# A fused attention and feed-forward kernel whose whole hand-recorded order, engine choice and buffer table are replaced by another

## The chip, the cores and the metric

The kernel runs on one core of one Trainium2 chip. The metric is the device time of one execution in microseconds (us); the profile's span runs from the first to the last instruction of the program. Five engines work side by side, each in its own order: PE (TensorE, matmuls), DVE (VectorE), ACT (ScalarE), POOL (GpSimd) and SP (SyncE, which here only issues DMAs). An engine never overtakes in its own queue: an instruction that waits holds up everything behind it on that engine.

## What is computed

Four batches with four heads of 1088 tokens (head size 32) go through an attention whose feature map is a product of two 8-row sketches, without softmax; the result, 4352 tokens of 128 values, goes through a two-layer network with a PReLU of 2048 channels.

```python
def phi(x):
    a = np.einsum('rd,bhsd->bhsr', S1, x)
    b = np.einsum('rd,bhsd->bhsr', S2, x)
    return np.einsum('bhsi,bhsj->bhsij', a, b).reshape(*x.shape[:-1], r * r)
q_p, k_p = (phi(q), phi(k))
kv = np.einsum('bhsf,bhsd->bhfd', k_p, v)
z = np.sum(k_p, axis=2)
num = np.einsum('bhsf,bhfd->bhsd', q_p, kv)
den = np.einsum('bhsf,bhf->bhs', q_p, z)[..., None] + 1e-06
x = (num / den)                      # 4352 tokens x 128
h = x @ w_in
g = np.maximum(h, 0.0) + alpha * np.minimum(h, 0.0)
out = g @ w_out
```

## The kernel before

The class `Graph` (line 43) makes a list of named steps; each has the engines on which it may run, the steps that it needs and its buffers. Nothing is scheduled when the kernel runs: the string `ORDER` (line 664) lists every step as `name@engine` (p PE, d DVE, a ACT, g POOL, s SP) and the loop at the end emits them in that order, so that each engine gets its own steps in the order of the string. `SLOTS` (line 655) says which of its class's buffers (PSUM banks among them) each logical buffer uses. Waits follow from the data and from buffers that are used again.

```python
    for word in ORDER.split():
        name, _, e = word.partition("@")
        if name in ("fill", "bit"):
            G.dummy(int(e), 512 if name == "fill" else 128)
            continue
        G.names[name].emit(E[e])
```

The names that the text uses, with b the batch (0 to 3):

- Loads on SP: `ld.kb.x`, `ld.qb.x`, `ld.vb.0` to `ld.vb.3` (keys, queries, values), `ld.w_in0` to `3` and `ld.w_out0` to `3` (weights, 256 KB each). A load into a padded or reused tile waits for a small memset first: `vpadb` (line 154) ahead of all loads of vb, `kpadb` (line 156) ahead of one load of kb, `hold.*` (line 159).
- Keys, `keys` (line 315 on): `kbT` transposes them (DVE, line 323), `kbf` is the sketch matmul, `kbab` transposes its result into the tile kab (DVE, line 333), `kbp..` are the key products, four for a batch (one a head, 576 wide; for batch 0 eight, of 320 or 256) on POOL or DVE into the tiles kp (line 134), `kbv` multiplies them with the values (PE), and `kbvc`, `kbvT`, `kbW` lead to the table kvW. `kbzm`, `kbcw`, `kbcc` make the denominator's weights fW.
- Queries: the first 512 tokens of batch 0 take a short way (`f0`, `f1`, line 397 on; tiles aq, dt, rr; `f0.x` writes the first activations xT). The others go `qbT`, `qbf` (PE), `qbg` (DVE, tile gt), `qbcb`, `qbs`, `qbe`, `qbrc`, `qbbd` (the denominator, tile dn), the four query products `qbp00` to `qbp11` (512 wide, POOL or DVE, tiles pr), two transposes `qbt0`, `qbt1` (DVE, line 480, tile pt), the numerators' matmul `qbn` (PE, tiles pt and kvW) and `qbx0`, `qbx2` (to xT).
- Weights, `weights` (line 268): `w_in_bf` casts; `w_a`, `w_b`, `w_hi`, `w_lo` (tiles wb, w_hl) make the PReLU's scaled copies of w_out; `winT`, `winTc`, `Wmm`, `W` make the product of both layers that carries alpha.
- The network, `mlp` (line 532): token blocks 0a, 0b (256 tokens), 1 to 6 (512) and 7 to 9 (256). For each of 16 channel chunks c: `hB.c` (PE, first layer into one PSUM bank), `rB.c` (relu to bf16 into one of ten rh tiles, ACT line 550 or DVE line 552), `oB.c` (PE, second layer); `WB` adds the alpha product, `tB` takes the result out, `sB` stores it. Blocks 7 to 9 are taken out by plain copies into the tiles oL, E and kvF.
- `warm`, `fill` and `bit` are matmuls on constants whose result nobody reads.

Blocks 0a, 0b and 1 hold batch 0; blocks 2 and 3 come out of q1 (batch 1), 4 and 5 out of q2, 6, 8 and 9 out of q3 and 7 out of the tokens left over in all batches.

Of the kernel before, what the change touches and what calls it, by code (L numbers as in the profile page):

```python
# [663 lines left out]
ORDER = """  # L664
ld.k0.0@s ld.rows1@s kpad0@g vpad2@g ld.k0.1@s ident@g mask4@d amkp@d par2@d q32@d hold.q2@g ld.w_in1@s k0T0@d zero@d ld.rows0@a warm@p ld.q0.0@s
amkq@d ld.w_in0@s identb@g M8T@g fill@2 bit@2 rowsT@p kW@d ld.alpha@a k0T1@d hold.k1@d hold.q1@d fill@5 bit@1 k0f@p am@g table@a aT@p fW@d Sab1@a
w_in_bf1@a M8@d E8@g ld.w_out0@s Sab0@d Mz@d alphaT@a hold.k2@d vpad1@g ld.w_out1@s k0ab@d k0z@p vpad0@g kpad2@g q0T0@d bit@3 f0.a@p ld.v0.0@s f0.b@p
k0zm@d omaT@d k0p02@g ld.v0.1@s w_in_bf0@a f0.ac@a k0p00@d k0p03@d k0p10@d fill@1 bit@1 winT0@p ld.v0.2@s ld.v0.3@s ld.w_in3@s k0p12@d k0fz@p S1x@p
hold.qr@d f0.m@d k0p01@g w_b1@d k0zz@d w_a0@a k0p11@g S1rep@d k0p13@g f1.a@p winTc0@a k0zc@d f1.b@p w_hi1@a bit@3 f0.den@p f1.ac@d ld.q0.1@s
ld.w_in2@s f0.dT@d w_in_bf3@a ld.k1.0@s ld.w_out3@s w_b0@g k0v0@p k0cw@p f1.m@d q0T1@d k0v1@p k0Vc@d kpad1@g f0.e@a w_hi0@a f0.rc@d w_lo1@g f1.den@p  # L670
k0vc@a w_a1@g ld.k1.1@s k0VT@p ld.w_out2@s w_in_bf2@a k0vT@p f1.dT@d k0V@d w_lo0@g f0.num@p k0cc@d ld.v2.0@s f0.rr@d f0.x@d q0f@p h0a.6@p q0g@d
ld.k2.0@s ld.k3.0@s q0cb@g ld.v3.1@s winT1@p ld.q1.0@s h0a.4@p ld.v1.1@s w_b3@g h0a.12@p k1T0@d ld.k2.1@s ld.v2.2@s f1.e@a w_a3@a r0a.6@a ld.k3.1@s
ld.v3.2@s k0W@a ld.v1.3@s ld.q2.0@s ld.v1.0@s h0a.14@p r0a.4@a f1.rc@d r0a.12@a winTc1@a w_hi3@a f1.rr@d o0a.6@p f1.num@p q0s@d f1.x@d w_b2@g k1f@p
o0a.12@p h0a.10@p k1ab@d o0a.4@p h0b.8@p h0a.8@p k1z@p w_hi2@a h0b.2@p h0b.12@p q0e@g q0rc@d w_a2@g r0a.14@d r0a.8@a o0a.14@p h0a.2@p k1zm@d w_lo2@d
r0b.8@a q0bd@d w_lo3@d h0b.6@p q0p01@d h0b.14@p o0a.8@p r0a.2@a h0a.0@p o0a.2@p r0a.10@a q0p00@g r0a.0@a r0b.12@a Wmm@p r0b.2@a r0b.6@a o0a.0@p
o0a.10@p h0b.0@p q1T@d h0b.10@p q0t0@d ld.v1.2@s ld.v2.1@s W_lo@a r0b.14@a k1cw@p W@d k2T0@d r0b.0@a r0b.10@a q0n@p W0a@p q0x0@a k2f@p k1cc@d t0a@d
k2ab@d q1f@p q1g@d o0b.14@p k1p00@g k1p01@g k1p03@g k1p02@g h1.0@p o0b.0@p k2p03@d o0b.6@p q1cb@d h0b.4@p h1.11@p W0b@p o0b.10@p h1.12@p r0b.4@a
r1.0@a h1.2@p h1.10@p h1.7@p r1.7@a h1.4@p ld.v2.3@s ld.q3.0@s k2p02@g k2p01@g o0b.8@p q1s@d o0b.4@p r1.4@d q1e@a r1.12@a h1.5@p q1rc@d h1.8@p
o0b.12@p o0b.2@p q3T@d r1.5@a q1bd@g r1.8@a q1p01@g t0b@d k2z@p k1v0@p h1.3@p h1.6@p q2T@d q1p11@d q1p00@d q1p10@d r1.11@a o1.11@p h1.14@p k2zm@d
# [90 lines left out]
```

## Time and profile before

| | us |
|---|---|
| median of 3 runs | 110.03 (109.38 to 110.6) |
| the profiled execution | 110.21 |
| its span | 108.3 |
| PE busy | 97.3 (90%) |
| DVE busy | 84.1 (78%) |
| ACT busy | 69.8 (64%) |
| POOL busy | 43.0 (40%) |

Instructions, their durations and what ended a wait are read from the timeline; a row `x2` merges neighbours. Matmuls overlap (each is shown with its time through the array), so PE's progress is read from the starts of two neighbours. The view by stages gives each engine's busy time between two moments. The last part of the chain of waits names only PE for most of the span, from 44.69 us to 103.91 us.

### The profile page before, as it was taken

How to read it: one execution, taken by the hardware profiler on the slowest of the kernel's cores; microseconds unless marked ns; L12 is line 12 of the kernel's file. 1: busy time of each engine (PE TensorE's matmuls, PEld its weight loads, DVE VectorE, ACT ScalarE, POOL GpSimd, SP SyncE). 2: the span in 40 equal slices, each digit the busy share in tenths (PEclk: the TensorE clock that was granted, in tenths of full speed). 3: DMA queues.
4: the chain of work that ended last, by engine and by line, in shares of the span. 5: the costliest groups of instructions: out<-in, count | busy, mean ns of one | idle time of the engine just before them, and what ended most of it. 6: DMA issues, size and time to landing. Idle time of an engine off the chain costs nothing.

```text
span 108.3 us, 3658 instructions
## 1 busy us (share of the span) xinstructions
PE 97.3 (90%) x1522; PEld 57.3 (53%) x1533; DVE 84.1 (78%) x151; ACT 69.8 (64%) x139; POOL 43.0 (40%) x58
## 2 busy tenths in 40 slices
PE   7998487899799899799999999999999999999950
PEld 2456254458646654544444444444644446699940
DVE  2499978879989999989978893779794594894810
ACT  3159666999924799338696448762994695658520
POOL 5449692856978380002960940026800230000000
PEclk9999999999999999999999999999999999999997
DMA  2897679997950000000510523250111000027333
GB/s 81 244 334 196 190 255 376 402 328 210 319 197 3 0 9 0 6 0 6 97 24 4 108 45 91 48 97 0 29 28 29 0 0 6 0 49 121 72 62 99
DMA packets 21730, 11.28 MB, mean 104 GB/s; under 512 B 16192, under 2 KB 19024, under 8 KB 21712
## 3 DMA queue, kind: packets, MB, share of 16 engines
q1 hardware_dynamic: 20808, 10.82, 35.7%
q10 hardware_dynamic: 904, 0.21, 0.8%
q8 instruction: 12, 0.20, 0.8%
q14 instruction: 6, 0.05, 0.1%
HBM read 8.80 MB, written 2.23 MB: 102 GB/s over the span
## 4 chain that ended last, share of the span: by engine, by line
PE 57%; DVE 21%; DMA 9%; issue 4%; POOL 3%; ACT 2%; SPq 1%; ACTq 1%; DVEq 0%
PE ps L137 56%; DMA w_out_f<-in_moe_w_out_dram 5%; DMA k<-in_k_dram 3%; DVE pt__78 L480 2%; DVE kp__70 L134 2%; DVE kT__64 L323 2%; DVE pr__76 L134 2%; POOL kp__69 L134 1%; POOL pr__75 L134 1%; DVE kp__69 L134 1%; DVE dn__80 L134 1%; DVE gt__73 L451 1%; DVE qT__72 L509 1%; DVE qT__71 L509 1%; ACT w_a L278 1%
## 5 line engine op out<-in xcount | busy, mean ns | idle before, releaser
L137 PEld LDWEIGHTS <-w_in_bf 128*128 128x128 bf16 x176 | 16.7, 98 | 13.0 <-issue 2.1
L137 PE MATMUL ps<-xT__103,w_in_bf 128*128 128x256 bf16 (+1 forms) x94 | 22.2, 325 | 0.4 <-issue 0.2
L137 PEld LDWEIGHTS <-w_a 128*128 128x128 bf16 x128 | 12.2, 98 | 12.4 <-issue 2.6
L137 PE MATMUL ps<-xT__104,w_in_bf 128*128 128x256 bf16 (+1 forms) x63 | 15.5, 325 | 0.2 <-issue 0.2
L550 ACT ACTIVATE rh__89<-ps 128x512 bf16<-128x512 f32 x16 | 9.6, 602 | 7.2 <-PE ps L137 7.0
L134 POOL TENSOR_TENSOR kp__69<-kab__66 128x576 f32<-128x576 f32 (+1 forms) x9 | 10.8, 1222 | 4.2 <-DVE kab__66 L333 4.2
L550 ACT ACTIVATE rh__88<-ps 128x512 bf16<-128x512 f32 x15 | 9.1, 605 | 3.5 <-PE ps L137 3.4
L550 ACT ACTIVATE rh__92<-ps 128x512 bf16<-128x512 f32 x13 | 7.9, 610 | 1.6 <-PE ps L137 1.4
L134 POOL TENSOR_TENSOR pr__75<-gt__73 128x512 f32<-128x512 f32 x7 | 7.8, 1121 | 2.4 <-DVE gt__73 L134 2.0
L134 POOL TENSOR_TENSOR dn__80<-gt__73 128x128 f32<-128x128 f32 (+2 forms) x3 | 1.5, 498 | 18.0 <-DVE gt__73 L451 18.0
L137 PE MATMUL ps<-pt__78,kvW 32*32 32x256 f32 (+2 forms) x320 | 6.9, 332 | 1.2 <-DVE pt__78 L480 0.6
L137 PE MATMUL ps<-const-bfloat16-1.0 128*128 128x512 bf16 (+1 forms) x24 | 6.3, 406 | 0.9 <-PEq L754 0.8
L550 ACT ACTIVATE rh__93<-ps 128x512 bf16<-128x512 f32 x9 | 5.5, 606 | 2.4 <-PE ps L137 2.3
L550 ACT ACTIVATE rh__90<-ps 128x512 bf16<-128x512 f32 x11 | 6.7, 606 | 0.5 <-PE ps L137 0.5
L137 PE MATMUL ps<-rh__88,w_a 128*128 128x512 bf16 (+1 forms) x21 | 6.5, 339 | 0.5 <-ACT rh__88 L550 0.5
L323 DVE STREAM_TRANSPOSE kT__64<-k 128x1152 f32<-128x1152 f32 (+1 forms) x5 | 5.6, 1129 | 1.5 <-DMA k<-in_k_dram 1.4
L137 PE MATMUL ps<-rh__89,w_a 128*128 128x512 bf16 (+1 forms) x21 | 6.1, 328 | 0.3 <-issue 0.2
L451 DVE STREAM_TRANSPOSE gt__73<-ps 128x1024 f32<-128x1024 f32 (+2 forms) x5 | 4.9, 984 | 1.8 <-PE ps L137 1.7
L137 PEld LDWEIGHTS ps<-pt__78,kvW 32*32 32x32 f32 x320 | 4.1, 103 | 3.7 <-DVE pt__78 L480 1.0
L550 ACT ACTIVATE rh__94<-ps 128x512 bf16<-128x512 f32 x9 | 5.6, 623 | 0.4 <-PE ps L137 0.4
L137 PE MATMUL ps<-rh__92,w_a 128*128 128x512 bf16 (+1 forms) x16 | 5.7, 366 | 0.1
L550 ACT ACTIVATE rh__91<-ps 128x512 bf16<-128x512 f32 x9 | 5.5, 609 | 0.3 <-PE ps L137 0.3
(202 smaller groups left out, 231.3 us busy)
## 6 DMA issues: line engine op xcount, KB each, us to landing
v<-in_v_dram SPq DMA_DIRECT2D x12, 144.0 KB, 4.5
q<-in_q_dram SPq DMA_DIRECT2D x3, 512.0 KB, 5.6
k<-in_k_dram SPq DMA_DIRECT2D x4, 288.0 KB, 6.3
k<-in_k_dram SPq DMA_DIRECT2D x4, 256.0 KB, 4.3
w_in_f<-in_moe_w_in_dram SPq DMA_DIRECT2D x4, 256.0 KB, 4.4
w_out_f<-in_moe_w_out_dram SPq DMA_DIRECT2D x4, 256.0 KB, 5.6
out_dram<-oT__100 SPq DMA_DIRECT2D x12, 64.0 KB, 1.9
q<-in_q_dram SPq DMA_DIRECT2D x2, 256.0 KB, 4.9
```

What stands on the lines that cost most here:

```text
L134: (self.nc.vector if e == "dve" else self.nc.gpsimd).tensor_tensor(out=dst, in0=a, in1=b, op=what)
L137: self.nc.tensor.matmul(out, w, x, start=start, stop=stop, skip_group_check=True)
L278: self.nc.scalar.activation(T[dst][:, c], T[f"w_out_f{i}"][:, c], ACTF.Copy, scale=T[a][:, 4 * i + c:4 * i + c + 1])
L323: turns.append(self.op(f"k{b}T{x}", [self.dvt(32 * NG * n)], lambda e, lo=lo, n=n: nc.vector.transpose(self.sb(bT, 32 * NG * lo, [1, 32 * ...
L451: o = self.op(tag + "g", [self.dvt(4 * n)], lambda e: nc.vector.transpose(self.sb(bG, 0, [n, 4], [1, n]), self.ps(bF, 0, [512, 4], [1, n]) ...
L480: ts.append(self.op(f"{tag}t{x}", [self.dvt(64 * g)], lambda e, bP=bP, x=x: nc.vector.transpose(self.sb(bPT, 64 * g * x, [1, 64 * g]), sel ...
L509: t = self.op(f"q{b}T", [self.dvt(1024)], lambda e: nc.vector.transpose(self.sb(bT), T[f"q{b}"]), L["q", b], [bT])
L550: nc.scalar.activation(self.sb(br), self.ps(bh, 0, [1, 512]), ACTF.Relu)
```

## The change

`SLOTS` and `ORDER` are replaced as a whole; no step is added to the work or taken from it, and the constant matmuls are listed otherwise (fewer short ones). The rest of the file is the same.

```diff
-SLOTS = [6, 4, 5, 1, 0, 1, 0, 6, 0, 3, 0, 0, 0, 0, 1, 6, 6, 0, 5, 5, 1, 0, 4, 1, 6, 0, 0, 0, 4, 0, 0, 0, 0, 0, 1, 0, 1, 1, 0, 1, 2, 0, 0, 0, 0, 0, 2,
+SLOTS = [6, 5, 5, 0, 0, 1, 1, 1, 2, 1, 0, 0, 0, 1, 0, 4, 4, 0, 5, 6, 0, 0, 4, 1, 6, 0, 0, 0, 5, 4, 0, 0, 0, 0, 1, 0, 5, 0, 0, 1, 0, 0, 0, 0, 0, 0, 0,
...
-ld.k0.0@s ld.rows1@s kpad0@g vpad2@g ld.k0.1@s ident@g mask4@d amkp@d par2@d q32@d hold.q2@g ld.w_in1@s k0T0@d zero@d ld.rows0@a warm@p ld.q0.0@s
+kpad0@g ident@g hold.qr@g ld.k0.0@s ld.rows1@s hold.q1@g ld.k0.1@s hold.k1@g identb@g amkq@d mask4@d par2@d zero@d warm@p ld.rows0@a ld.q0.0@s
...
```

By engine, the steps that change their place between engines are: key products, from 14 on POOL and 6 on DVE to 17 and 3; query products, from 9 on POOL and 5 on DVE to 12 and 2; `w_lo` from two on each to three on POOL and one on DVE, `w_b` from three on POOL and one on DVE to four on POOL; `w_a` from two on ACT and two on POOL to three and one; `winTc` both from ACT to DVE; relus from 81 on ACT and 39 on DVE to 78 and 42; `f1.ac` and `k0Vc` from DVE to ACT; `q1x2` and `q2x2` from DVE to ACT and `q2x0` from ACT to DVE; `vpad1`, `vpad2`, `kpad1` and `kpad2` from POOL to DVE, four of the `hold` memsets from DVE to POOL and one back. `vpad0`, for which the values of batch 0 wait, stays on POOL, where it now stands ahead of `E8` and `am` and before stood behind them and behind `vpad1`.

On SP, the loads at the start of the program stand so before (k0, q0, v0 are batch 0; names carry the tile's number):

```order
L143 DMA k0_141<-in_k_dram 128x576
L143 DMA rows_113<-in_S2_dram 8x4x32
L143 DMA k0_141<-in_k_dram 128x512
L143 DMA w_in_f1_151<-in_moe_w_in_dram 128x512
L143 DMA q0_144<-in_q_dram 128x512
L143 DMA w_in_f0_150<-in_moe_w_in_dram 128x512
L143 DMA w_out_f0_154<-in_moe_w_out_dram 128x512
L143 DMA w_out_f1_155<-in_moe_w_out_dram 128x512
L143 DMA v0_147<-in_v_dram 32x4x288 x3
L143 DMA v0_147<-in_v_dram 32x4x224
L143 DMA w_in_f3_153<-in_moe_w_in_dram 128x512
L143 DMA q0_144<-in_q_dram 128x512
```

And so after:

```order
L143 DMA k0_141<-in_k_dram 128x576
L143 DMA rows_113<-in_S2_dram 8x4x32
L143 DMA k0_141<-in_k_dram 128x512
L143 DMA q0_144<-in_q_dram 128x512
L143 DMA w_in_f3_153<-in_moe_w_in_dram 128x512
L143 DMA v0_147<-in_v_dram 32x4x288
L143 DMA w_out_f1_155<-in_moe_w_out_dram 128x512
L143 DMA v0_147<-in_v_dram 32x4x288 x2
L143 DMA v0_147<-in_v_dram 32x4x224
L143 DMA w_in_f2_152<-in_moe_w_in_dram 128x512
L143 DMA q0_144<-in_q_dram 128x512
L143 DMA w_out_f3_157<-in_moe_w_out_dram 128x512
```

Ahead of the last value load stand two weight loads where five stood (four of them ahead of the first).

On POOL, from the last weight step up to the end of batch 1's query products, before (kp are key products, pr query products, dn and gt the denominator):

```order
L134 TENSOR_TENSOR w_a2_166<-w_out_f2_156,omaT_120 128x512
L134 TENSOR_TENSOR pr0__75<-gt0__73 128x512
L134 TENSOR_TENSOR kp0__69<-kab0__66 128x9x64 x4
L134 TENSOR_TENSOR kp1__70<-kab1__67 128x9x64 x2
L134 TENSOR_TENSOR gt0__73<-gt0__73,dn0__80 128x32x8
L134 TENSOR_TENSOR pr0__75<-gt0__73 128x512
L134 TENSOR_TENSOR kp1__70<-kab1__67 128x9x64
```

After:

```order
L134 TENSOR_TENSOR gt0__73<-gt0__73,dn0__80 128x16x8
L134 TENSOR_TENSOR pr0__75<-gt0__73 128x512 x2
L134 TENSOR_TENSOR w_a2_166<-w_out_f2_156,omaT_120 128x512
L134 TENSOR_TENSOR kp0__69<-kab0__66 128x9x64 x4
L134 TENSOR_TENSOR kp1__70<-kab1__67 128x9x64 x2
L131 TENSOR_SCALAR dn0__80<-dn0__80 128x32
L134 TENSOR_TENSOR kp1__70<-kab1__67 128x9x64
L134 TENSOR_TENSOR gt0__73<-gt0__73,dn0__80 128x32x8
L134 TENSOR_TENSOR pr0__75<-gt0__73 128x512 x2
L134 TENSOR_TENSOR pr1__76<-gt0__73 128x512
L134 TENSOR_TENSOR kp1__70<-kab1__67 128x9x64
L134 TENSOR_TENSOR pr1__76<-gt0__73 128x512
```

Both of batch 0's query products, all of batches 1 and 2's key products and all four of batch 1's query products are now POOL's; before, five of them were DVE's.

On ACT, the last steps of the program before (the tile oL1 is block 9's first half, E8 block 8's first, oL0 block 8's second):

```order
L122 COPY E8_128<-ps_63 128x128
L550 ACTIVATE rh5__93<-ps_63 128x512
L550 ACTIVATE rh7__95<-ps_63 128x512
L550 ACTIVATE rh4__92<-ps_63 128x512
L578 DMA out_0_dram<-oL0__101 32x4x128
L122 COPY oL1__102<-ps_63 128x128
L578 DMA out_0_dram<-oL1__102 32x4x128
```

After (here oL0 is block 8's first half, oL1 its second, kvF block 9's first):

```order
L122 COPY oL0__101<-ps_63 128x128
L550 ACTIVATE rh0__88<-ps_63 128x512
L578 DMA out_0_dram<-oL0__101 32x4x128
L578 DMA out_0_dram<-oL1__102 32x4x128
L122 COPY kvF_131<-ps_63 128x128
L578 DMA out_0_dram<-kvF_131 32x4x128
```

One relu of the last block stands there where three did, and both of block 8's stores are ACT's now. On PE, nine matmul steps stand behind the last one of block 8's second half, and three behind the last one of block 9's second half; before, thirteen and four.

More of the change, by code (lines that the diff above doesn't have):

```diff
@@ L668 @@
[L668 to L679, printed above, removed]
@@ new lines @@
+o1.5@p o1.4@p o1.6@p o1.15@p q1p00@g q1p01@g h1.3@p q2g@d W1@p h1.1@p o1.9@p h1.14@p r1.3@a q1p11@g k2p02@g ld.k3.0@s q1t0@d s0a.1@s h1.11@p k1vT@p
+k2v0@p r1.0@a k1W@a r1.14@a k2vc@a r1.1@a q1p10@g q2cb@g o1.0@p o1.2@p q1t1@d r1.11@a k3T0@d r1.8@d q2s@d q2e@g o1.10@p o1.14@p o1.3@p o1.7@p q1n@p
+q1x0@a k3f@p q2rc@d k3ab@d o1.8@p o1.1@p q1x2@a h2.6@p h2.8@p h2.11@p h2.2@p q2bd@g q2p00@g k3p01@g q2p01@g r2.8@a r2.6@a h2.3@p h2.0@p r2.3@a o1.13@p
+o1.11@p h2.9@p r2.2@a r2.0@d t1@d h2.15@p k3z@p k2vT@p r2.9@d h2.14@p k3zm@d r2.14@d h3.10@p o2.2@p h2.1@p h3.2@p q2p11@g k3p00@g r2.11@a k2W@a qrT@d
```

62 lines of the change are left out of this document (35 added, 27 removed), and 16 rows, old and new, of the table SLOTS.

## The prediction

> **What bounds the kernel now.** I read the page's busy line first, then the view by stages, then the timeline where a stage begins or ends, and the chain of waits only to see where it leaves PE. The stages below are cut at the moments that the order's steps mark: the first value matmul (13.76), the first matmul of the network (18.48), the reciprocal of q0 (23.45), the numerators of q1 (44.69), the first matmul on q1's tokens (47.65) and PE's end (104.3). The columns are the stage, its length, then busy us and instructions of PE, PEld, DVE, ACT, POOL, the clock and the DMA share.
>
> ```profile
> PE 97.3 (90%) x1522; PEld 57.3 (53%) x1533; DVE 84.1 (78%) x151; ACT 69.8 (64%) x139; POOL 43.0 (40%) x58
> ...
> 13.76:18.48 4.72, 3.70 (x149) 2.48 (x142) 3.67 (x11) 3.29 (x6) 3.23 (x3) 1.00 0.88 306
> 18.48:23.45 4.97, 4.51 (x58) 2.65 (x58) 3.89 (x7) 4.70 (x11) 3.74 (x5) 1.00 1.06 387
> 23.45:44.69 21.24, 19.26 (x387) 13.14 (x387) 20.67 (x32) 15.67 (x33) 12.14 (x10) 1.00 0.34 106
> 44.69:47.65 2.96, 2.91 (x100) 1.57 (x101) 2.56 (x4) 0.59 (x1) 0.00 (x0) 1.00 0.00 0
> 47.65:104.30 56.65, 55.93 (x688) 31.40 (x687) 43.19 (x70) 38.01 (x75) 15.47 (x18) 1.00 0.22 41
> 104.30:108.30 4.00, 0.00 (x0) 0.00 (x0) 0.14 (x1) 0.27 (x1) 0.00 (x0) 0.83 0.42 99
> ```
>
> The busy line alone would say PE. The stages say more: from 47.65 on PE is busy 55.93 of 56.65 us, and the time there can only go down by work done earlier. In the 21 us before, DVE is busy 20.67 of 21.24 us, and PE (whose busy time counts overlaps) has to wait for it. So the end is the moment at which q1's tokens are there, plus PE's work that is then left, plus the tail.
>
> **The first stage, to the first value matmul (13.76).**
>
> ```profile
> 6.72 0.56 POOL L154 MEMSET v<- 128x256 f32 x2
> 7.31 2.71 SPq L143 DMA_DIRECT2D v<-in_v_dram  x4
> 7.87 1.74 POOL L134 TENSOR_TENSOR kp__69<-kab__66 128x320 f32<-128x320 f32 x2 [0.49 <-DVE kab__66 L333]
> 8.53 1.43 DVE L134 TENSOR_TENSOR kp__69<-kab__66 128x320 f32<-128x320 f32 x2
> 9.57 1.64 POOL L134 TENSOR_TENSOR kp__70<-kab__66 128x256 f32<-128x256 f32 x2
> 9.88 1.61 DVE L134 TENSOR_TENSOR kp__70<-kab__66 128x256 f32<-128x256 f32 x2
> 13.76 0.77 PE L137 MATMUL ps<-kp__69,v 128*32 128x64 f32 x40
> ```
>
> The loads of the values waited on SP for vpad0, whose POOL memset ended at 7.28; they went out from 7.31 on. The key products were done at 11.49 (DVE), so the 13.76 is the values' landing. Now vpad0 is among POOL's first steps and two weight loads of 256 KB stand ahead of the last value load instead of five: the values are there before the products. The products set the start: POOL has five of them at (1.74 + 1.64)/4 = 0.84, from 7.87 to 12.1; DVE has three, at (1.43 + 1.61)/4 = 0.76, but between them and behind q0's transpose five small steps and a 512-wide product, some 1.5 together, so 8.5 + 2.3 + 1.5 = 12.3. I take 12.3: 1.5 us earlier. If the values land no earlier it is 0, the upper end.
>
> **From there to the network (4.72) and to q0's reciprocal (4.97).** The steps stay; the copy k0Vc goes to ACT, and DVE's wait for q0's second half goes, since that load stands ahead of two weight loads more.
>
> ```profile
> 10.95 0.99 ACT L122 COPY winT<-ps 128x1024 bf16<-128x1024 bf16 x1
> ...
> 15.73 0.71 DVE L512 STREAM_TRANSPOSE qT__71<-q 128x512 f32<-128x512 f32 x1 [0.77 <-DMA q<-in_q_dram]
> ...
> 18.52 0.72 DVE L451 STREAM_TRANSPOSE gt__73<-ps 128x512 f32<-128x512 f32 x1
> ```
>
> But q0g (0.72) now stands ahead of f0.rr and f0.x on DVE, and takes the 0.77 back: 4.7, first network matmul at 17.0. In the next stage DVE, busy 3.89 of 4.97, gets winTc twice; no row has it on DVE, its 0.99 on ACT is the nearest, so 2.0 at most and 0 if it fits into the 1.08 idle. It loses q0g and f1.rr and f1.x (half as wide as q0g, about 0.45 each) go behind q0rc, 1.6 together: 5.2, and q0rc starts at 22.2 instead of 23.45.
>
> **The long stage, q0rc to q1's numerators (21.24).** Both costs of moving products from DVE to POOL are in these rows.
>
> ```profile
> 25.09 0.69 DVE L134 TENSOR_TENSOR w_hl<-wb__111,w_hl 128x512 bf16<-128x512 f32 x1
> 25.25 1.45 POOL L134 TENSOR_TENSOR pr__75<-gt__73 128x512 f32<-128x512 f32 x1 [2.03 <-DVE gt__73 L134]
> 25.70 1.55 DVE L134 TENSOR_TENSOR pr__75<-gt__73 128x512 f32<-128x512 f32 x1
> 33.93 0.75 DVE L134 TENSOR_TENSOR kp__70<-kab__67 128x576 f32<-128x576 f32 x1
> 37.46 0.63 POOL L134 TENSOR_TENSOR gt__73<-gt__73,dn__80 128x256 f32<-128x256 f32 x1 [1.74 <-DVE dn__80 L459]
> 38.17 1.07 POOL L134 TENSOR_TENSOR pr__75<-gt__73 128x512 f32<-128x512 f32 x1
> 39.20 1.19 POOL L134 TENSOR_TENSOR kp__70<-kab__67 128x576 f32<-128x576 f32 x1
> 39.80 1.14 DVE L134 TENSOR_TENSOR pr__76<-gt__73 128x512 f32<-128x512 f32 x1
> 41.46 0.68 DVE L134 TENSOR_TENSOR pr__76<-gt__73 128x512 f32<-128x512 f32 x1
> 42.17 1.25 DVE L480 STREAM_TRANSPOSE pt__78<-pr__76 128x1024 f32<-128x1024 f32 x1
> 44.69 1.48 PE L137 MATMUL ps<-pt__78,kvW 32*32 32x256 f32 x64 [0.59 <-DVE fW L358]
> 50.14 0.29 POOL L131 TENSOR_SCALAR dn__80<-dn__80 128x32 f32<-128x32 f32 x1 [9.76 <-DVE dn__80 L455]
> ```
>
> DVE loses q0p01 (1.55), w_lo3 (0.69), k2p03 (0.75) and three of q1's products (1.14 and two of 0.68): 5.5 us. It gets three relus more (0.68 each, as wide as those products), f1.rr and f1.x (0.9), q2g (1.25, as q1t1) and loses q3T (1.2, as wide as q2g) and q0bd (0.3): 20.67 - 5.5 + 2.0 + 0.9 - 0.25 = 17.8.
> POOL gets the chain, and nothing on it may be overtaken: q0bd (0.6 at most), two q0 products (2.1), w_a2 (1.07, like any 512), eight key products (9.5), q1e (0.3, and some 0.5 of waiting for DVE's q1s ahead of it), q1bd (0.63), four q1 products (4.3): 19.0. Beside it DVE has w_lo2 (0.69) and q1cb left that read two tiles of SBUF; in the rows, a POOL product beside w_hl took 1.45 for 1.07. I take half of 1.1 for these two, 0.55; 0 and 1.1 are the ends. POOL so ends at 22.2 + 19.5 = 41.7, behind it q1t1 (1.25), and q1n starts at 43.0, 1.7 earlier. The bound changes: POOL, with 40% of the span, sets this stage now, DVE has 2 us of slack.
>
> The Trainium skill, page "SBUF — State Buffer", section "Who interferes with whom", speaks against moving products there: a DVE instruction with two SBUF inputs and a GpSimd one that reads SBUF do not share, the second waits until the first is done. The trace agrees: 25.09 + 0.69 is 25.78, and 1.07 behind that is 26.85, where the POOL row ends at 26.70. By that rule each collision costs POOL the whole rest of DVE's instruction, 1.1 instead of my 0.55, and the sum below would be 107.4, which lies within the forecast's own ends and has its chance there.
>
> **From q1n to the first matmul on its tokens (2.96).**
>
> ```profile
> 46.18 0.59 ACT L122 CAST xT__103<-ps 128x512 bf16<-128x512 f32 x1 [1.64 <-PE ps L137]
> ...
> 46.86 0.86 PE L137 MATMUL ps<-qT__72,fW 32*32 32x256 f32 x32
> ...
> 47.65 0.39 PE L137 MATMUL ps<-xT__103,w_in_bf 128*128 128x512 bf16 x1
> ```
>
> In this place q2f (0.86) kept PE from h2; it now stands before q1n, and k3f stands here with two second-layer matmuls, so 1.48 + 0.71 + 0.4 = 2.6: h2 at 45.6, 2.05 earlier.
>
> **The dense stage (56.65).**
>
> ```profile
> 49.17 0.38 PE L137 MATMUL ps<-rh__91,w_a 128*128 128x512 bf16 x1
> ...
> 49.38 0.38 PE L137 MATMUL ps<-rh__92,w_a 128*128 128x512 bf16 x1
> ...
> 57.77 0.71 PE L137 MATMUL ps<-kT__64,kW 64*32 64x288 f32 x16
> ```
>
> Behind h2 stood six second-layer matmuls of block 1 (0.21 apart, 1.3) and k3f (0.7); now two (0.4) and k2vT (0.4): 1.2 less work. Against it both casts of q1's tokens are ACT's, so its first relu comes one cast (0.6) later while DVE still has k3T0 and q2s; I charge 0.6, the ends are 0 (seven PSUM banks cover it) and 1.2 (a second relu late). 56.65 - 1.2 + 0.6 = 56.05.
>
> **The tail (4.0).**
>
> ```profile
> 103.95 0.29 DVE L124 COPY oL__101<-ps 128x128 f32<-128x128 f32 x1 [1.18 <-PE ps L137]
> 104.01 0.28 PE L137 MATMUL ps<-w_a,rh__95 128*128 128x128 bf16 x2
> 104.28 0.65 ACTq L578 DMA_DIRECT2D out_dram<-oL__101  x1
> ...
> 105.10 0.27 ACT L122 COPY oL__102<-ps 128x128 f32<-128x128 f32 x1 [1.73 <-DVE kvF L124]
> ```
>
> The last copy, t9a on ACT, could have started at 104.3 and started at 105.10, behind the issue of s8b, which waited for t8b. Block 8's second half now ends nine matmuls (1.0) ahead of PE's end, so the issue (0.65) is nearly over by then: 0.7 less; 0 if t8b waits again, 0.8 at most.
>
> **Sum.** 110.21 (span 108.3 and 1.9 around it) - 2.05 (q1's tokens) - 1.2 + 0.6 (work left, first relus) - 0.7 (tail) = 106.9. The 1.5 of the first stage is in the 2.05, not beside it. The profiled execution is 0.2 over the median of the runs (110.03), so against that 106.9 is 3.1 less.
>
> **Rivals.** *The values gain nothing* (the change does not do what its first part says): if the first stage still ends at 13.76, everything to q1n shifts back by up to 1.5: 108.4, still faster. For it: all DMAs share one queue that is at 0.88 to 1.06 from 13.76 on. Against: fewer bytes stand ahead.
> *The lead is given back in the dense stage.* DVE and ACT together are busy 81.2 of 113.3 there, 72%; POOL takes the products of q2 and q3 too, and relus that come late stop PE at 0.6 each. Four such stops take 2.4: 109.3, within 1%.
> *POOL's chain makes it slower.* Its steps from q0rc to q1p10 follow each other without slack, and products that collide cost 0.4 more (1.45 for 1.07), those that wait for a step of DVE behind a relu 0.7. All fourteen at 0.4, with four such waits, are 8.4 instead of 1.05: 106.9 + 7.3 = 114.2. From about 4 us of added wait on the chain (ten collisions) the kernel is no longer faster, from 5.3 on slower by over 1%; halfway it stands at 111.5. For it: the products on POOL in the old trace had 1.7 of waits ahead of them (37.46). Against: DVE's colliding products are gone.
>
> **Chances.** About 1% is what a measurement of this kernel can tell from no change (108.9 and 111.1). My forecast 0.55, values gain nothing 0.13 (both faster); lead given back 0.19 (same); POOL's chain 0.13 (slower). So faster 0.68, same 0.19, slower 0.13. The forecast's own ends: collisions 0.55 either way, the relus 0.6 either way, winTc and the products 0.5 each, together 105.0 to 108.6. The range reaches to the second rival and half a microsecond beyond, 105.0 to 109.8; above it 0.14 and below 0.06 are left.
>
> **What would show it.** The first value matmul at 12 to 12.6 and its last wait a key product, not a DMA; the first network matmul at 17.0; POOL busy over 18 of the 21 us ahead of q1n, and q1n at 43.0 behind q1t1 behind a POOL product; first h2 at 45.6; PE busy over 98% from there; t9a within 0.2 of PE's end. Wrong it is if q1n starts later than 44 (POOL), if PE shows idle gaps of 0.3 and more behind relus after 46 (dense stage), or if DVE waits for w_in, w_out or k1 loads before 20, whose issue on SP now stands behind kpad1 and vpad2 on a busy DVE.

## The result, and the profile after

| | us |
|---|---|
| before, median of 4 runs beside it | 110.05 (109.38 to 110.6) |
| after, median of 4 runs | 106.53 (106.47 to 106.99) |
| after over before | 0.9672, 95% interval 0.9636 to 0.9708 |
| the profiled execution of after, and its span | 106.47, 104.6 |

The forecast was 106.9. Ratios and medians, here and below, leave out the executions that ran over 1.5% above the fastest of the same kernel.

The busy line of the page of after stands first here, then the view by stages, cut at the same six moments as in the prediction (stage, its length, then busy us and instructions of PE, PEld, DVE, ACT and POOL, the clock, the DMA share, GB/s).

```profile
PE 95.2 (91%) x1517; PEld 56.1 (54%) x1531; DVE 77.4 (74%) x149; ACT 68.5 (66%) x137; POOL 48.3 (46%) x65
```

```profile
0.00:10.90 10.90, 9.83 (x131) 5.02 (x132) 7.31 (x25) 4.81 (x10) 6.62 (x21) 1.00 0.77 237
10.90:17.05 6.15, 3.79 (x165) 2.54 (x160) 4.07 (x15) 5.11 (x9) 4.41 (x6) 1.00 0.90 295
17.05:21.33 4.28, 4.08 (x65) 2.64 (x63) 4.07 (x9) 3.79 (x10) 3.91 (x4) 1.00 0.97 356
21.33:42.11 20.78, 20.46 (x423) 13.76 (x425) 18.02 (x30) 15.62 (x35) 18.91 (x19) 1.00 0.48 151
42.11:44.63 2.52, 2.47 (x83) 1.20 (x83) 2.07 (x5) 1.17 (x3) 0.44 (x2) 1.00 0.02 7
44.63:99.95 55.32, 54.60 (x662) 30.95 (x668) 41.34 (x69) 37.77 (x73) 13.99 (x16) 1.00 0.18 32
99.95:104.60 4.65, 0.00 (x1) 0.00 (x0) 0.49 (x2) 0.27 (x1) 0.00 (x0) 0.79 0.46 95
```

Two stages grew: the second (4.72 before, 6.15 now), where PE is busy 3.79 us only, and the tail (4.0 before, 4.65 now). All others shrank, the first most (13.76 to 10.90). In the fourth, before, DVE was busy 20.67 of 21.24 us; now three engines are busy for 87% of it or more, PE most of all (20.46 of 20.78).

The chain of waits (start, length, what), read in order of time, tells which of the three it is:

```profile
13.90 5.02 DMA w_out_f<-in_moe_w_out_dram
...
19.05 1.05 POOL wb__112 L134
...
20.12 0.63 ACT w_hl L122
20.75 0.66 DVE winT L124
...
21.46 9.65 PE ps L137 x196
...
97.31 3.13 DMA out_dram<-oL__102
...
100.51 0.29 DVE oL__102 L124
...
101.43 0.27 ACT kvF L122
```

Up to 21.46 the chain runs over a weight load and the steps on its data; from 21.46 to 93.49 nearly every piece is PE's. Before, that began at 44.69. So the change brought forward, by 23 us, the moment from which the chain stays on PE. At the end the chain leaves PE and waits 3.13 us for a store to have left the tile oL1.

The timeline at the start of after, first what ends the products, then PE up to the copy that turns the key-value sums (k0VT, line L382):

```profile
9.88 1.46 POOL L134 TENSOR_TENSOR kp__69<-kab__66 128x256 f32<-128x256 f32 x2
10.14 0.71 DVE L134 TENSOR_TENSOR kp__70<-kab__66 128x320 f32<-128x320 f32 x1
...
10.90 0.77 PE L137 MATMUL ps<-kp__70,v 128*32 128x64 f32 x40
...
12.04 0.45 PE L137 MATMUL ps<-aq__82,zc 64*32 64x128 f32 x16
...
14.48 0.33 PE L382 MATMUL ps<-ident,fs__109 128*128 128x128 f32 x1 [1.99 <-ACT dt__84 L129]
```

The first value matmul starts 0.05 us behind the last product of its group (10.14 + 0.71), not behind a load. Then PE stands still for 1.99 us. The step named as its releaser had ended at 13.55, and k0VT does not read its result, so the name is no explanation; the experiments look for one.

The timeline of the tail of after, of the tiles oL0 and oL1, kvF and the stores' issues:

```profile
95.08 1.13 SPq L578 DMA_DIRECT2D out_dram<-oT__100  x2
95.66 0.28 DVE L124 COPY oL__102<-ps 128x128 f32<-128x128 f32 x1
96.72 1.45 SPq L578 DMA_DIRECT2D out_dram<-oL__102  x2
...
100.51 0.29 DVE L124 COPY oL__102<-ps 128x128 f32<-128x128 f32 x1 [2.09 <-DMA out_dram<-oL__102]
100.84 0.55 ACTq L578 DMA_DIRECT2D out_dram<-oL__102  x1
101.43 0.27 ACT L122 COPY kvF<-ps 128x128 f32<-128x128 f32 x1 [3.03 <-DVE E L124]
```

t7b filled oL1 at 95.94. Its store s7b was issued at 96.72, since SyncE was at work on a store of block 4 (oT, 95.08) whose data had been there for 22 us, and it had left at 100.44. Only then could t8b fill oL1 again. ACT stood at the issue of s8b, which waits for t8b, and t9a, behind it, started 1.48 us after PE's end.

### The profile page after: what moved, and what is told of

It reads as the page before. It is cut to its first block, busy times and chain, and to the rows that moved or that the text cites. A ratio compares the mean times of both kernels' runs of the same rounds, so it can differ in the third digit from the quotient of the medians.

```text
span 104.6 us, 3655 instructions
## 1 busy us (share of the span) xinstructions
PE 95.2 (91%) x1517; PEld 56.1 (54%) x1531; DVE 77.4 (74%) x149; ACT 68.5 (66%) x137; POOL 48.3 (46%) x65
## 4 chain that ended last, share of the span: by engine, by line
PE 75%; DMA 8%; SPq 5%; DVE 4%; issue 2%; ACT 2%; POOL 1%; ACTq 0%; DVEq 0%; POOLq 0%
PE ps L137 74%; DMA w_out_f<-in_moe_w_out_dram 5%; DMA out_dram<-oL__102 3%; SPq L578 3%; SPq L143 2%; POOL wb__112 L134 1%; DVE aq__82 L416 1%; DVE winT L124 1%; ACT w_hl L122 1%; DVE kp__70 L134 1%; DVE rh__91 L552 1%; ACT aq__82 L122 1%; PE ps L391 1%; DVE kvW L124 0%; ACTq L578 0%
## 5 line engine op out<-in xcount | busy, mean ns | idle before, releaser
L137 PE MATMUL ps<-xT__103,w_in_bf 128*128 128x512 bf16 (+1 forms) x111 | 28.0, 333 | 0.3 <-issue 0.2
L137 PEld LDWEIGHTS <-w_in_bf 128*128 128x128 bf16 x176 | 16.2, 98 | 12.6 <-issue 2.1
L137 PEld LDWEIGHTS <-w_a 128*128 128x128 bf16 x128 | 12.3, 98 | 12.6 <-issue 1.7
L137 PE MATMUL ps<-xT__104,w_in_bf 128*128 128x256 bf16 (+1 forms) x63 | 14.9, 326 | 0.1
L550 ACT ACTIVATE rh__88<-ps 128x512 bf16<-128x512 f32 x13 | 7.8, 597 | 7.0 <-PE ps L137 6.9
L550 ACT ACTIVATE rh__89<-ps 128x512 bf16<-128x512 f32 x15 | 9.0, 599 | 4.6 <-PE ps L137 4.6
L134 POOL TENSOR_TENSOR kp__69<-kab__66 128x576 f32<-128x576 f32 (+1 forms) x11 | 11.4, 1053 | 1.0 <-DVE kab__66 L333 0.9
L550 ACT ACTIVATE rh__90<-ps 128x512 bf16<-128x512 f32 x12 | 7.1, 596 | 1.6 <-PE ps L137 1.1
L550 ACT ACTIVATE rh__92<-ps 128x512 bf16<-128x512 f32 x9 | 5.4, 602 | 1.3 <-PE ps L137 1.3
L552 DVE TENSOR_SCALAR rh__91<-ps 128x512 bf16<-128x512 f32 x7 | 4.7, 672 | 1.9 <-PE ps L137 1.6
L550 ACT ACTIVATE rh__93<-ps 128x512 bf16<-128x512 f32 x9 | 5.4, 601 | 0.8 <-PE ps L137 0.7
L550 ACT ACTIVATE rh__94<-ps 128x512 bf16<-128x512 f32 x9 | 5.4, 600 | 0.6 <-ACT rh__92 L550 0.4
L137 PE MATMUL ps<-rh__88,w_a 128*128 128x256 bf16 (+1 forms) x20 | 5.7, 326 | 0.1
L122 ACT CAST w_in_bf<-w_in_f 128x512 bf16<-128x512 f32 x4 | 4.5, 1122 | 1.7 <-DMA w_in_f<-in_moe_w_in_dram 1.7
L480 DVE STREAM_TRANSPOSE pt__78<-pr__75 128x1024 f32<-128x1024 f32 (+1 forms) x5 | 5.6, 1112 | 0.0
L137 PE MATMUL ps<-rh__89,w_a 128*128 128x512 bf16 (+1 forms) x16 | 5.3, 353 | 0.0
```

The lines of the kernel that those rows point to most:

```text
L122: nc.scalar.copy(dst, src)
L134: (self.nc.vector if e == "dve" else self.nc.gpsimd).tensor_tensor(out=dst, in0=a, in1=b, op=what)
L137: self.nc.tensor.matmul(out, w, x, start=start, stop=stop, skip_group_check=True)
L480: ts.append(self.op(f"{tag}t{x}", [self.dvt(64 * g)], lambda e, bP=bP, x=x: nc.vector.transpose(self.sb(bPT, 64 * g * x, [1, 64 * g]), sel ...
L550: nc.scalar.activation(self.sb(br), self.ps(bh, 0, [1, 512]), ACTF.Relu)
L552: nc.vector.tensor_scalar_max(self.sb(br), self.ps(bh, 0, [1, 512]), 0.0)
```

## The experiments

Each kernel's ratio is to the kernel before, measured beside it on the same chip; the changed kernel's is 0.9672 above and 0.9724 in run 5. The spread between those two is as large as several of the effects below, so the readings rest on marks of the profiled execution, one for each kernel. Edits of `ORDER` are shown as excerpts, `...` for what is left out; steps that are only shifted within a line are not all shown.

**1. The values late.**

```diff
-am@g k0T1@d ld.v0.0@s ld.w_out1@s S1rep@d ld.v0.1@s
+am@g k0T1@d ld.w_out1@s S1rep@d
...
-k0zm@d ld.v0.2@s ld.v0.3@s ld.w_in2@s
+k0zm@d ld.w_in2@s
...
-k0p12@g k0v0@p
+k0p12@g ld.q0.1@s ld.w_out3@s ld.w_in1@s ld.v0.0@s ld.v0.1@s ld.v0.2@s ld.v0.3@s k0v0@p
```

> The changed kernel with the four loads of batch 0's values put back behind six weight loads' worth of SyncE issues (w_in2, w_out3, w_in1 and q0's second half now go ahead of them), all else as it is. The last value load should land at 12.8 us instead of before 9.5, so the first value matmul comes at about 13.0 instead of 10.90. Theory A (the lead carries through): every mark behind it moves by 2.1, the first network matmul to 19, and the kernel takes 108.5. Theory B (PE stood still from 12.52 to 14.48 ahead of k0VT for a reason that has nothing to do with the values, a fetch of its instructions): the second value matmuls end at 14.3, k0VT comes at 14.8 to 15 instead of 14.48, the first network matmul at 17.4 instead of 17.05, and the kernel takes 106.6 to 107.0.

Ratio 0.9757 (0.9678 to 0.9835), median 108.43. On PE's timeline the first value matmul, and in the view by stages the two microseconds around it:

```profile
14.14 1.29 PE L137 MATMUL ps<-kp__70,v 128*32 128x64 f32 x40 [3.00 <-DMA v<-in_v_dram]
```

```profile
14.00:16.00 2.00, 1.86 (x72) 1.89 (x72) 0.00 (x0) 0.00 (x0) 0.00 (x0) 0.51 0.88 301
```

The values landed at 14.0, later than I had expected, the first value matmul came 3.2 us later than in the changed kernel, the reciprocal of q0 2.56 later (23.89), q1's numerators 2.57 (44.68), PE's end 2.55. So theory A: what the values' delay is worth at q0's reciprocal, 2.56, stays to the end. Of the 3.2 at the first value matmul 0.7 is gone by then, by two things of opposite sign: PE has no stop ahead of k0VT here, and it works more slowly. It had been idle for 3.0 us, its clock fell to 0.51, and the same 40 matmuls took 1.29 us instead of 0.77. In the profiled executions the whole is 2.4 of the change's 3.7 us (108.91 against 106.47); by the ratios it is less, and their intervals overlap.

**2. Only the values early, in the kernel before.**

```diff
-ld.k0.0@s ld.rows1@s kpad0@g vpad2@g ld.k0.1@s
+ld.k0.0@s ld.rows1@s kpad0@g vpad0@g vpad2@g ld.k0.1@s
...
-k0z@p vpad0@g kpad2@g
+k0z@p kpad2@g
...
-ld.q0.0@s amkq@d ld.w_in0@s
+ld.q0.0@s ld.v0.0@s ld.v0.1@s ld.v0.2@s ld.v0.3@s amkq@d ld.w_in0@s
```

> The kernel before with nothing changed but the values: vpad0 is POOL's second step and the four value loads stand directly behind q0's first half. The first value matmul should come at 11.6, behind the last key product (11.49), instead of 13.76. Theory A (the lead carries through, as the prediction's sum had it): the first network matmul comes about 1.5 to 2 earlier than 18.48 and the kernel takes 108.5. Theory B (the copy k0Vc stands on DVE behind the transpose of q0's second half, which waits for a load that lands at 15.7 either way): k0Vc stays at 16.4, the first network matmul at 18.4, and the kernel takes 110.0, as before. Then the values' early loads are worth nothing without the other moves.

Ratio 1.01 (1.0051 to 1.015), median 111.71: 1% slower than before, which neither theory said. ACT's timeline and PE's:

```profile
11.37 1.09 ACT L122 CAST w_in_bf<-w_in_f 128x512 bf16<-128x512 f32 x1 [2.95 <-DMA w_in_f<-in_moe_w_in_dram]
12.37 0.58 ACT L122 COPY aq__82<-ps 128x512 f32<-128x512 f32 x1
```

```profile
12.51 1.03 PE L299 MATMUL ps<-identb,w_in_bf 128*128 128x128 bf16 x8 [2.62 <-ACT w_in_bf L122]
...
16.70 1.29 PE L137 MATMUL ps<-kp__69,v 128*32 128x64 f32 x40
```

In the old order PE turns the first weights (winT0, L299) ahead of f1.a, f0.den and the value matmuls. Four value loads ahead of w_in0 make its cast late, PE waits 2.62 us for the cast, its clock falls (0.57 from 12 to 14), and the value matmuls come at 16.70. In this place the early values do not pay; the change has other things beside them: the weights used first are other ones (w_in3, w_out1), and winT0 stands behind the value matmuls.

**3. Five products back on DVE.**

```diff
-q0p01@g
+q0p01@d
...
-k2p03@g
+k2p03@d
...
-q1p00@g q1p01@g
+q1p00@d q1p01@g
...
-q1p11@g
+q1p11@d
...
-q1p10@g
+q1p10@d
```

> The changed kernel with five products given back to DVE: q0p01, k2p03, q1p00, q1p11 and q1p10. Theory A (the prediction's: DVE bound this stage before and POOL's chain does now): DVE gets 4.8 us more of work in a stage in which it had some 2 of slack, q1's numerators start at 43.5 to 45 instead of 42.11, and the kernel takes 108 to 109. Theory B (PE or the loads set q1's numerators, the split is worth little): 42.1 and 106.5, within 0.3.

Ratio 0.9742 (0.966 to 0.9823), median 108.35; by the ratios alone it can't be told from the changed kernel (0.9724 in run 5). The profiled execution took 110.29, and its PE clock was at 0.67 and 0.50 from 16 to 20 us; the stage that matters lies behind that, at full clock:

```profile
23.28:45.98 22.70, 21.04 (x427) 13.77 (x426) 21.98 (x35) 15.48 (x35) 14.82 (x14) 1.00 0.40 126
```

From q0's reciprocal to q1's numerators it takes 22.70 us, against 20.78 in the changed kernel (21.25 in its second profile; 20.78 to 21.67 in all ten profiles that leave these products and w_a2 on POOL). DVE is busy 21.98 of the 22.70, and PE is idle for 1.66, where it is idle for 0.32 in the changed kernel. Theory A: DVE is the bound again, for 1.5 to 1.9 us.

**4. One step less in POOL's chain.**

```diff
-w_a2@g
+w_a2@a
```

> The changed kernel with w_a2 (1.0 us on POOL, between q0's and batch 1's products) on ACT. Theory A (POOL's chain from q0's reciprocal to the last of q1's products sets this stage): that chain ends 1.0 earlier, at 39.2 instead of 40.19, q1's numerators start at 41.1 instead of 42.11, and the kernel takes 105.5. Theory B (something else sets it): 106.5, or 107 where ACT's extra 1.2 us delays relus.

Ratio 0.9692 (0.9607 to 0.9778), median 107.94. The stage took 22.26 us. Part of that is not the edit's: POOL's w_b2, just ahead of the stage, waited longer for its weight load, here (first view) and in the second profile of the changed kernel (second view), than the 0.25 us of its first profile.

```profile
20.49 1.04 POOL L134 TENSOR_TENSOR wb__112<-w_out_f,alphaT 128x512 f32<-128x512 f32 x1 [1.18 <-DMA w_out_f<-in_moe_w_out_dram]
```

```profile
20.40 1.04 POOL L134 TENSOR_TENSOR wb__112<-w_out_f,alphaT 128x512 f32<-128x512 f32 x1 [0.93 <-DMA w_out_f<-in_moe_w_out_dram]
```

Counted from the end of w_b2, the numerators start 22.32 us later here (43.85) and 21.60 later there (43.04): the edit gained nothing and cost 0.7. By the view of waits for POOL (what, total us, times, longest):

```profile
POOL dn__80 L131 <- DVE dn__80 L455: 1.4, 1, 1.4
```

POOL was through with the key products at 32.48 and then waited 1.4 us at q1e for DVE's q1s, which hangs on q1f of PE (30.60); w_a2 and behind it w_a3 on ACT made PE's steps ahead of q1f late (q0n, counted from the end of w_b2 again, 7.15 instead of 6.51). So theory B: take POOL's work away and give it to ACT, and the wait goes to another engine. That POOL's microsecond would be worth nothing if ACT didn't get it is not shown by this run.

**5. The changed kernel once more.** No instruction is edited.

> The changed kernel once more, unaltered, as the measure for the three beside it: 106.5 to 107.5. In the profiles so far k0f, PE's first matmuls on the keys, started at 5.8 in two runs and at 7.0 in two others, without any other difference ahead of it; the six constant matmuls ahead of it took 0.22 us apart there and 0.43 apart here, that is, the PE clock had or hadn't risen. Either is expected here.

Ratio 0.9724 (0.9654 to 0.9793), median 107.22; k0f at 6.94, against 5.78 in the first profile. The six constant matmuls ahead of it in the first profile of the changed kernel:

```profile
3.94 1.48 PE L137 MATMUL ps<-const-bfloat16-1.0 128*128 128x512 bf16 x6
```

and in the second:

```profile
4.09 2.50 PE L137 MATMUL ps<-const-bfloat16-1.0 128*128 128x512 bf16 x6
```

The same six take 1.48 us where the clock has risen and 2.50 where it hasn't, and the keys' matmuls start behind them. With it go the first value matmul (12.06 instead of 10.90), q1's numerators (43.04 instead of 42.11) and the profiled time (107.22 instead of 106.47); no other difference of that size shows ahead of them.

**6. and 7. PE's stop: fewer, and more, constant matmuls.**

```diff
-Sab0@a fill@6 S1x@p
+Sab0@a S1x@p
...
-k0f@p bit@3 aT@p
+k0f@p aT@p
...
-f0.m@d fill@3 f1.a@p
+f0.m@d f1.a@p
...
-f0.den@p fill@1 k0VT@p
+f0.den@p k0VT@p
```

> The changed kernel without thirteen of its constant matmuls (26 PE instructions: the six ahead of S1x, three short ones behind k0f, three ahead of f1.a, one ahead of k0VT). Theory A (PE stands still from 12.52 to 14.48 because its next instructions are not there: the 16 KB instruction fetch that begins at 12.13 comes too late): the stop follows the count of instructions, so k0VT runs without it, at 12.7 to 12.9 instead of 14.48, and the stop lies some 22 instructions later, in q0f, up to 1.4 to 1.5 behind the end of that fetch. Theory B (k0VT waits for something of its own: its copy on ACT, its bank): the stop stays ahead of k0VT. Also, k0f should start at 5.7 whatever the PE clock does, where it starts at 5.8 or 7.0 with the six. Time: 106.0 to 106.5 against a control of 106.5 to 107.5, unless PE's clock falls for want of work (then 107 and more).

```diff
-Sab0@a fill@6 S1x@p
+Sab0@a bit@24 S1x@p
...
-f0.m@d fill@3 f1.a@p
+f0.m@d bit@12 f1.a@p
```

> The changed kernel with nine of its 512-wide constant matmuls cut into 36 of 128 columns: as many columns, 54 PE instructions more. Theory A (instruction fetch): the stop lies 54 instructions earlier in the program, inside the second value matmuls k0v1 or in f0.den, and k0VT follows f0.den without a stop; time about the same, 106.5 to 107.5. Theory B: the stop stays ahead of k0VT.

With fewer the ratio is 0.979 (0.9712 to 0.9869): k0f came at 5.91, but the matmuls behind it ran at half pace (the 40 value matmuls in 1.38 us, from 13.02), k0VT came at 15.89, and there is no stop; a slow PE had no need of one, so this run decides nothing about it. With more constant matmuls the ratio is 0.9815 (0.9732 to 0.9898). PE's timeline:

```profile
11.74 0.51 PE L137 MATMUL ps<-kp__69,v 128*32 128x64 f32 x22
14.78 0.63 PE L137 MATMUL ps<-kp__69,v 128*32 128x64 f32 x10 [2.53 <-issue]
```

The stop is now inside one step, between its 22nd and its 23rd matmul, where nothing but the instructions themselves can be waited for ("issue" is what the profile says where it sees no releaser). Counted up to the stop, PE had executed as much as in the changed kernel, by the view by stages (matmuls and weight loads of the first 12.52 us, and here of the first 12.25):

```profile
0.00:12.52 12.52, 11.42 (x219) 6.34 (x221) 8.68 (x31) 6.43 (x13) 8.24 (x23) 1.00 0.81 256
```

```profile
0.00:12.25 12.25, 11.28 (x221) 7.44 (x221) 8.42 (x30) 5.87 (x11) 7.72 (x22) 1.00 0.77 254
```

440 and 442: the stop follows the count, not the step. The program says the same: between the two places lie ten value matmuls, the sixteen of f0.den and one constant matmul, each with its weight load, which makes 54 instructions, as many as the edit had added. (The text ahead of run 8 counts 447 to 449; the view by stages gives 440 or 442 in all eight profiles that stop in this way.) Theory A.

**8. The instructions' fetch early.** PE's warming matmuls cut into 112 small ones; the three fewer ahead of S1x keep the keys from waiting.

```diff
-self.pe(3030)], lambda e: self.dummy(7), ni=14)
+self.pe(3030)], lambda e: self.dummy(112, 32), ni=14)
...
-            self.mm(self.T["PS"][:, 7, :k], one(128), one(k))
+            self.mm(self.T["PS"][:k if k < 128 else 128, 7, :k], one(min(k, 128)), one(k))
...
-Sab0@a fill@6 S1x@p
+Sab0@a fill@3 S1x@p
```

> The changed kernel with its seven 512-wide warming matmuls cut into 112 of 32 columns (as many columns, 210 PE instructions more) and three instead of six constant matmuls ahead of S1x. In six profiles PE stopped behind its 447th to 449th recorded instruction, and went on 1.4 to 1.5 us after the first 16 KB fetch was through. Theory A (PE executes that many instructions out of what is there, and asks for more when it has used up a part of them): with 210 more ahead of the keys, that fetch starts before 9 us instead of at 12.1 to 13.0, the 449th instruction falls in f1.a at about 10.4 and finds its followers there, k0VT follows f0.den at 12.7 to 13.0 (k0f at 5.7) without a stop over 0.6, the first network matmul comes at 15.7 to 16.4, and the time falls by 0.5 to 1.3 against the changed kernel. Theory B (the fetch is held up by the loads until 12, whenever it is asked for): the stop moves ahead to f1.a, from 10.4 to 14, and the kernel is 1 to 2 slower.

Ratio 0.9814 (0.9767 to 0.9861). The DMA view of the tenth of a microsecond in which the first 16 KB fetch starts, from 12.1 in the changed kernel:

```profile
q8 instruction: 1, 0.02, 55.0%
```

and from 4.75 here:

```profile
q8 instruction: 1, 0.02, 60.1%
```

So the fetch went out at 4.80 with 210 more instructions ahead and at 12.13 without. With 54 more, in run 7, it went out no earlier (12.36), so what starts it is not settled. PE has no idle stretch over 0.6 us at the start, once it has begun. The gain is not there all the same, by PE's timeline and the view by stages:

```profile
12.67 1.30 PE L137 MATMUL ps<-kp__70,v 128*32 128x64 f32 x40
```

```profile
12.00:14.00 2.00, 2.00 (x84) 1.67 (x72) 1.22 (x4) 0.83 (x2) 1.47 (x2) 0.50 0.89 298
```

PE's clock fell to half from about 8 to 15, and k0VT came at 15.50. A slow PE had no stop in run 6 either, so its absence here proves little. That the stop follows the count of instructions is shown by run 7; that an earlier fetch removes it, and that a kernel without it is faster, are not shown.

**9. The tail: stores earlier, tiles of their own, and both.**

```diff
-s3.1@s r5.9@d
+s3.1@s s4.0@s r5.9@d
...
-s5.0@s r6.14@a
+s5.0@s s5.1@s r6.14@a
...
-s6.0@s o7a.12@p
+s6.0@s s6.1@s o7a.12@p
```

> The changed kernel with three stores issued earlier on SyncE: s4.0 right behind s3.1, s5.1 behind s5.0, s6.1 behind s6.0 (their data is there 10 to 20 us before they were issued). Theory A (the tail is as long as it is because t8b waits for oL1 until s7b has left it, and s7b stood on SyncE behind s4.0): s7b is issued at PE's end less 4.0 instead of less 3.2, its data has left by PE's end less 1.5 instead of plus 0.5, t8b starts at PE's end less 1.0 instead of plus 0.56, t9a within 0.2 of PE's end instead of plus 1.48, and the kernel is 1.2 to 1.5 faster than the control. Theory B (the last stores wait for ACT or the landing of small stores whatever stands ahead): the tail stays at 4.3 to 4.7 us behind PE's end, and the time as the control's.

Ratio 0.9762 (0.9681 to 0.9843). s7b was issued at once, 4.0 us ahead of PE's end (101.56), and yet:

```profile
97.59 1.18 SPq L578 DMA_DIRECT2D out_dram<-oL__102  x2
...
101.67 0.29 DVE L124 COPY oL__102<-ps 128x128 f32<-128x128 f32 x1 [1.62 <-PE ps L137]
```

The store had left at 101.55 only; its last four packets started 0.6 us behind all others, about when a 16 KB instruction fetch that had begun at 99.47 ended (it took 1.09). t9a started 1.03 behind PE's end, and the tail was 4.1. (PE's clock was at 0.51 and 0.64 from 16 to 20 us in this profile, so its whole time, 107.5, says nothing of the tail.) Neither theory in full: SyncE's order was one cause, and behind it the wait stayed.

```diff
-    T["oL"] += [T["E8"], T["kvF"]]
+    T["oL"] += [T["E8"], T["kvF"], T["S1rep"], T["Sab"]]
```

In `SLOTS`, t8a and t8b have the tiles 4 and 5 (S1rep, Sab) instead of 0 and 1.

> The changed kernel with a tile of its own for each of the six last outputs: two long-dead constants' tiles (S1rep, Sab) join the four, so t8a and t8b need not wait until the stores of t7a and t7b have left theirs. Nothing else differs. Theory A (the tail is set by t8b's wait for oL1, whatever holds up the store s7b: SyncE's order, or as in the run with the earlier stores four packets that stand behind an instruction fetch): t8b starts at PE's end less 1.0 instead of plus 0.5, s8b is off ACT before PE ends, t9a starts within 0.2 of PE's end instead of plus 1.4, and the tail behind PE's end is 3.0 to 3.3 instead of 4.65; the time falls by 1.3 to 1.5 against the changed kernel (ratio to before 0.955 to 0.96). Theory B (the landing of the last stores sets it: three stores are issued at once then): the tail stays above 4.2.

Ratio 0.9684 (0.9635 to 0.9733). On the timeline, the last steps:

```profile
99.98 1.29 SPq L578 DMA_DIRECT2D out_dram<-oT__98  x2
99.99 0.27 ACT L122 COPY kvF<-ps 128x128 f32<-128x128 f32 x1 [1.63 <-PE ps L137]
...
101.36 0.57 SPq L578 DMA_DIRECT2D out_dram<-E  x1
```

t9a starts at PE's end (99.95), as expected, but s9b, the store of E8, now stands behind s5.1 on SyncE and goes out at 101.36. The tail is 4.25: one wait is gone, the next was behind it. With both edits:

> The changed kernel with both tail edits and nothing else: a tile of its own for each of the six last outputs, and the stores s4.0, s5.1 and s6.1 issued 10 to 20 us earlier on SyncE. With own tiles alone t9a started at PE's end, but the store s9b stood behind s5.1 on SyncE and was issued 1.4 us behind PE's end. Theory A (two things held the tail, each of which hides the other: the tile of t8b, and SyncE's order): the last issue ends at PE's end plus 0.9, the tail behind PE's end is 3.2 instead of 4.65 in the changed kernel and 4.2 with own tiles alone, and the time is 1.3 to 1.5 below the changed kernel's, 105.0 to 105.9, ratio to before 0.953 to 0.962. Theory B (the tail is already short enough with own tiles; the earlier stores are worth nothing): tail 4.2, ratio 0.964 to 0.970.

Ratio 0.9512 (0.9438 to 0.9586), median 104.86, the fastest of all. The tail, in the view by stages:

```profile
100.13:103.30 3.17, 0.00 (x0) 0.00 (x0) 0.00 (x0) 0.27 (x1) 0.00 (x0) 1.00 0.22 62
```

Theory A: 3.17 instead of 4.65, with the last issue ended 0.88 behind PE's end. Edits 8 and 9 together:

> Both edits, own tiles for the last six outputs and the warming matmuls cut up, with the three earlier stores beside them. If both theories A hold the gains add up: 2 to 2.7 faster than the changed kernel, 104 to 104.8, ratio to before 0.945 to 0.952. If the fetch's does not, as own tiles alone or slower.

Ratio 0.9656 (0.9626 to 0.9686), median 106.35: the tail was 3.2 there too, and the clock that the small warming matmuls cost took most of it back.

## Why the prediction was right, and where not

| stage, up to | before | forecast | after |
|---|---|---|---|
| first value matmul | 13.76 | 12.3 | 10.90 |
| first network matmul | 4.72 | 4.7 | 6.15 |
| q0's reciprocal | 4.97 | 5.2 | 4.28 |
| q1's numerators | 21.24 | 20.8 | 20.78 |
| first matmul on q1's tokens | 2.96 | 2.6 | 2.52 |
| PE's end | 56.65 | 56.05 | 55.32 |
| end (tail) | 4.0 | 3.3 | 4.65 |

The time came out 0.4 us under the forecast because errors of both signs nearly cancel: -1.4, -0.9 and -0.7 against +1.45 and +1.35. So close a hit is luck; what holds is the direction, and that q1's tokens come 3.0 us earlier (44.63 instead of 47.65). One sum of the forecast does not come out either: its four ends (0.55, 0.6 and twice 0.5) make 2.15 either way, 104.75 to 109.05, not 105.0 to 108.6.

- **First stage.** The mechanism was right: the values are there first, and the last key product of the first group releases the value matmul. Run 1 shows that the lead goes through to the end, so the rival that the values gain nothing falls. The size was off. For 8.5 + 2.3 + 1.5 on DVE the rows have 7.96 for the start, 1.74 for its three products (0.48, 0.55 and 0.71) and 1.15 between them, which ends at 10.85. The start depends on PE's clock: in the second profile of the changed kernel the mark stands at 12.06.
- **To the network.** "The steps stay" left out that PE can run out of instructions. Bringing the value matmuls forward, close behind f1.a, put 185 matmuls and weight loads into 1.62 us, and the fetch that began at 12.13 came too late for what follows them (run 7). Before, the first fetch began at 10.53, and by 14.80 PE had used only 405. The view by stages of after, from the first value matmul to the stop:

```profile
10.90:12.52 1.62, 1.59 (x96) 1.33 (x89) 1.36 (x7) 1.62 (x4) 1.62 (x3) 1.00 1.07 383
```

- **To q0's reciprocal.** The term was mis-sized. I had let in up to 2.0 of DVE's work (the two winTc), taken 1.6 out, and charged 0.2 more than before. The work came out about so: DVE is busy 4.07, before 3.89, and the winTc took 0.68 and 0.65. But it went into DVE's idle time (1.08 before, 0.21 now), the case that I had put at 0, and the stage is 0.7 shorter. By the chain it hangs on a weight load now, whose issue had waited on SyncE behind vpad1 and kpad1 of a busy DVE, much as the prediction warned; it cost POOL 0.25 us at w_b2, and 0.93 in the second profile.
- **The long stage.** The length was right (20.78 for 20.8), and DVE's new sum too (18.02 for 17.8). Run 3 shows that the products on DVE were the old bound. The step that failed is "POOL, with 40% of the span, sets this stage now". POOL's chain took 18.86 us from the reciprocal, not 19.5, and the numerators started 0.64 behind the last transpose, because PE was at other work. PE, busy 20.46 of 20.78, had become the bound: in its order it had 0.32 us of idle time left, so an earlier end of POOL could have brought the numerators forward by no more than that. Run 4 agrees, as far as it goes. The view by stages of before could not show it, since PE waited there; PE's work that the new order moves into the stage had to be added up too (19.26 before, 20.46 after).
- **Collisions.** I charged 0.55 for two. Beside DVE's q1cb two key products took 2.53, where two of the four ahead of them take 2.31 (half of 4.61), so 0.2. Beside w_lo2 (DVE, 21.48 to 22.11) q0bd took longer than q1bd, which is twice as wide:

```profile
21.64 0.73 POOL L134 TENSOR_TENSOR gt__73<-gt__73,dn__80 128x128 f32<-128x128 f32 x1 [0.43 <-DVE dn__80 L459]
...
34.19 0.63 POOL L134 TENSOR_TENSOR gt__73<-gt__73,dn__80 128x256 f32<-128x256 f32 x1
```

  That is at least 0.1, and about 0.4 if half the width takes half of 0.63 (an estimate). So the charge was about right. By the rule in the Trainium skill, "SBUF — State Buffer", section "Who interferes with whom", the second instruction would lose the whole overlap with q1cb (31.20 to 31.55, 0.35); here it lost less.
- **The dense stage.** The work moved out of it was sized right (1.33 less for 1.2); the 0.6 for the late first relus was not due. PE is busy 54.60 of 55.32, so the late cast cost nothing, which was the lower end that I had given; that it was the seven banks that covered it is likely, not tested.
- **The other rivals.** Neither came. PE's longest wait in the dense stage is 0.2 us, so the lead was not given back there; POOL's steps took no added 0.4 each, so its chain did not make the kernel slower.
- **The tail.** Here the prediction was wrong, in the step "Block 8's second half now ends nine matmuls (1.0) ahead of PE's end, so the issue (0.65) is nearly over by then: 0.7 less; 0 if t8b waits again, 0.8 at most." t8b's operand was ready at 98.95, 1.0 ahead of PE's end as forecast; its tile was not, for SyncE and the store's own way out (run 9). The new slots put t8b into the tile that t7b had just filled, and no row of before spoke of that tile; the order and the slots did. With both causes taken away the tail is 3.17, near the forecast's 3.3.

## What to carry to other kernels

A stage's bound is not the engine that got the moved work, but the one whose sum is largest after the move: add up every engine, PE with all that the new order brings into the stage. A store that is issued late holds its tile, and the tile's next user holds its engine's queue; give the last outputs tiles of their own and issue finished stores before it matters, both, since each hides the other. A load moved forward pushes others back: ask which waiting engine queue stands on those.
